# Moving PSUM copies to ScalarE and reordering work around the transposes in a fused attention and mixer kernel

## Chip, cores and metric

One NeuronCore of a Trainium2 chip. The metric is the device time of one execution in microseconds, median of repeated runs; all runs compared here are in the fast state (one single run, v_alone, can't be assigned); the granted TensorE clock is 0.99 to 1.00 of full speed in all of them.

## The reference

For 8 batches of 8 heads (sequence 576, head dimension 64) it computes causal attention with a bias made of a running sum, puts the heads together, and sends the result through a low-rank mixer over the sequence and a two-layer channel mixer:

```python
scores = q @ k.T / 8                                   # per batch and head
cum    = cumsum(max(s, 0))
scores = where(causal, -1e9, scores + minimum(-(cum_i - cum_j), 0))
x      = softmax(scores) @ v                           # heads side by side: [8, 576, 512]
u      = x + (x^T @ U @ V)^T                           # U: 576x32, V: 32x576
out    = u + relu(u @ w_ch1) @ w_ch2                   # 512 -> 2048 -> 512
```

## The kernel before

The work is cut into 32 pairs of heads; pairs 0 to 3 are batch 0, 4 to 7 batch 1, and so on. For a pair `n`, `T` transposes q and k on TensorE into PSUM, and four copies bring the result into an SBUF "slot"; `S` makes the scores and their exps, `V` the values. The channel mixer of an earlier group is cut into "chunks" of four 512-column matmuls, and `step_fill` slips them between the steps of attention so that TensorE always has something to do. An eviction, below, is a copy of a matmul's result out of PSUM, the memory that the matmuls of this kernel write to; exps and relus on ScalarE are evictions too.

The parts that matter here:

```python
ps_s = tile_pool(bufs=2, space=PSUM)   # pscore: two tiles of 1024 columns
ps_w = tile_pool(bufs=4, space=PSUM)   # pwork: four tiles of 512 columns, used in turn

def copies(n, hh, par):                # which engine copies a pair's transposes
    on_act = hh == 0 and (n in (0, 1, PB, PB + 1, PB + 3) or n == 2 and par == 0)  # PB = 4
    return nc.scalar.copy if on_act else nc.vector.tensor_copy

def transposes(n):                     # for b > 0: one yield for each head hh
    for hh in range(2):
        turn(hh, 0); turn(hh, 1)       # 8 transposes into one pwork tile
        for par in range(2):
            copies(n, hh, par)(dst[..., par], tp[par * D : par * D + D]...)   # 64x576 each
        yield
# ... cut ...
    step(M2)                           # M0..M3: the mixer of batch 0, one generator a head pair
    hidden_first(0)                    # hidden_first(kt): first four hidden tiles, step kt
    step(M3)
    hidden_first(1)
    step(M3)
    hidden_first(2)
    hidden_first(3)                    # ends with two 128x1024 relus on ScalarE (line 818)
    mix_first_end()
    in_program_order(tc, traced, [E.DVE, E.Activation, E.SP])
# ... cut ...
    for dt in range(4):                # V_sb and V_end: seven small copies on VectorE
        ...
    fill.append(chanmix(0, first_hT, 4))
    fill_with(3)                       # three chunks
    pace[1] = 8                        # from here one chunk at every second step
    weave("T4 T4 S4 T5 S4 T5 S4 S4")
    fill_with(5)
    pace[1] = 6
    weave("S5 S5 T6 S5 T6 S5 S6 R0 T7 S6 R1 T7 S6 R2 S6")   # R: v of batch 1, (act, dve) copies
```

The order in which TensorE runs its instructions is the order of the program text. The later order on VectorE and ScalarE is fixed at build time by a scheduler.

The softmax here doesn't subtract the row's maximum and nothing guards it: scores larger than these inputs give would overflow.

## Time and profile before

| | before |
|---|---|
| median | 382.94 us (382.32 to 383.56, 3 runs) |
| span of the profiled run | 381.3 us |
| TensorE busy | 371.3 us, 97% |
| VectorE busy | 223.6 us |
| ScalarE busy | 194.6 us |

From the page of the kernel before: the span, TensorE's busy line, the engines' shares of the chain that ended last, and the group of VectorE's slot copies (busy us and mean ns of one behind the first bar; behind the second, idle time before them and what ended it).

```profile
span 381.3 us, 8511 instructions
...
PE 371.3 (97%) x3583; PEld 210.8 (55%) x3583; DVE 223.6 (59%) x461; ACT 194.6 (51%) x292; POOL 65.1 (17%) x103
...
PE 85%; DVE 8%; ACT 3%; DMA 2%; issue 1%; SPq 0%; DVEq 0%; ACTq 0%
...
L310 DVE COPY slot<-pwork 64x576 bf16<-64x576 bf16 x117 | 93.6, 800 | 12.0 <-PE pwork L293 9.4
```

TensorE is the limit. But a matmul's recorded duration overlaps with the next one (the four at 111.88 us are recorded as 1.03 us long, and the next group starts after 0.87), so 97% busy hides gaps. The better measure is the time from one matmul's start to the next, less the rate at which matmuls of that size run when nothing is in the way. For that rate I took a line that fits the median spacings in the trace of the kernel before (216 ns at 512 columns, 135 at 320, 56 at 128, 29 at 64): N / 2.4 + 2.5 ns for N columns, at least 27 ns (32 columns take 25; without that floor the sum of waits below is 14.90 instead of 14.89). I call what lies above it (excesses over 20 ns) the PE waits. This stretch of the timeline gives the rate (start us, duration us, engine, line, operation, shapes, count): 64 matmuls of 512 columns in 13.81 us from first start to next group's start (322.97), 216 ns each.

```profile
309.16 13.98 PE L640 MATMUL pwork<-w_sb,hT 128*128 128x512 bf16 x64
```

Summed over a trace, by stretch of time:

| PE waits, us | 0-26 | 26-60 | 60-90 | 90-125 | rest | all |
|---|---|---|---|---|---|---|
| before | 5.28 | 3.30 | 2.74 | 1.26 | 2.31 | 14.89 |

The two waits that the change aims at look like this. First TensorE's, then ScalarE's timeline of the kernel before. In brackets stands the idle time of the engine and what ended it; that idle time starts at the modelled end of the matmul before, and so is shorter than the wait counted from starts (0.79 against 0.95 us here).

```profile
36.67 0.29 PE L293 MATMUL pwork<-identity,q_sd 72*128 72x72 bf16 x4
...
37.19 1.03 PE L630 MATMUL pwork<-uT,w_sb 128*128 128x512 bf16 x4
39.01 0.61 PE L375 MATMUL pscore<-slot 68*128 68x128 bf16 x6 [0.79 <-ACT slot L310]
```

```profile
33.66 1.94 ACT L818 ACTIVATE hT<-pscore 128x1024 bf16<-128x1024 f32 x2 [0.76 <-PE pscore L630]
...
37.37 1.59 ACT L310 COPY slot<-pwork 64x576 bf16<-64x576 bf16 x2
```

Pair 4's first transposes are done at 37.2 us, ScalarE copies them from 37.37 to 38.96, and the scores (line 375) start at 39.01. Later TensorE waits for VectorE's copies of pairs 8, 9 and 10, or for the evictions of x queued behind them. Five rows of TensorE's timeline of before:

```profile
68.70 0.62 PE L435 MATMUL pwork<-v_slot,hT 128*128 128x65 bf16 x15 [0.40 <-DVE slot L310]
...
75.27 1.04 PE L640 MATMUL pwork<-w_sb,hT 128*128 128x512 bf16 x4 [0.30 <-DVE slot L310]
...
77.52 0.62 PE L375 MATMUL pscore<-slot 68*128 68x128 bf16 x6 [0.28 <-DVE slot L310]
...
87.41 0.30 PE L293 MATMUL pwork<-identity,q_sd 72*128 72x72 bf16 x4 [0.15 <-DVE slot L310]
...
88.16 1.04 PE L630 MATMUL pwork<-uT,w_sb 128*128 128x512 bf16 x4 [0.32 <-DVE x_sb L445]
```

Counted from starts these five are 0.57, 0.46, 0.43, 0.31 and 0.48 us, 2.25 together.

The busy time of each engine from 60 to 90 us, for the kernel before (window in us; then PE, PEld, DVE, ACT, POOL busy us with counts; granted clock, DMA share, GB/s):

```profile
60.00:90.00 30.00, 28.55 (x399) 19.13 (x398) 25.16 (x55) 12.97 (x19) 4.19 (x6) 1.00 1.05 117
```

From 60 to 90 us VectorE is busy 25 of 30 us and ScalarE 13.

### The profile page before, as it was taken

The page shows a single profiled execution, that of the slowest core. Times are in us where ns is not written, and L with a number is a line of the kernel's source. Part 1 is how long each engine was busy: PE and PEld are TensorE (multiplying, and loading weights), DVE is VectorE, ACT ScalarE, POOL GpSimd, SP SyncE. Part 2 cuts the span into 40 slices and gives each one's busy share as a digit, 9 for nine tenths or more (in the row PEclk, how much of TensorE's full clock was granted, in tenths as well). Part 3 has the DMA queues.
Part 4 walks back from the last instruction along what each step waited for, and adds up shares of the span by engine and source line. Part 5 has one row for each costly group of instructions (what it writes and reads, how often), then busy time and mean ns, then how long its engine had stood idle before and what let it go on. Part 6 is the DMA issues. An engine that isn't in the chain of part 4 may idle for free.

```text
span 381.3 us, 8511 instructions
## 1 busy us (share of the span) xinstructions
PE 371.3 (97%) x3583; PEld 210.8 (55%) x3583; DVE 223.6 (59%) x461; ACT 194.6 (51%) x292; POOL 65.1 (17%) x103
## 2 busy tenths in 40 slices
PE   8899999999999999999999999999999999999997
PEld 3574456665665656555655665666555544444444
DVE  8883457977778776777668766786663132002002
ACT  3876985356642576247723774357542530630620
POOL 8995216005000600060006000000000000000000
PEclk9999999999999999999999999999999999999999
DMA  7999999937993994399239923320323032301002
GB/s 109 169 205 200 199 169 113 154 81 106 137 49 90 161 143 39 79 173 146 32 30 200 164 36 58 86 80 18 58 63 99 20 64 76 83 29 68 14 29 83
DMA packets 86110, 37.29 MB, mean 98 GB/s; under 512 B 66424, under 2 KB 80472, under 8 KB 86072
## 3 DMA queue, kind: packets, MB, share of 16 engines
q0 software_dynamic: 47216, 18.44, 49.0%
q1 hardware_dynamic: 38856, 18.31, 25.6%
q8 instruction: 28, 0.46, 0.5%
q14 instruction: 10, 0.08, 0.1%
HBM read 37.25 MB, written 9.70 MB: 123 GB/s over the span
## 4 chain that ended last, share of the span: by engine, by line
PE 85%; DVE 8%; ACT 3%; DMA 2%; issue 1%; SPq 0%; DVEq 0%; ACTq 0%
PE pwork L630 30%; PE pwork L640 29%; PE pscore L375 10%; PE pwork L435 6%; DVE slot L310 3%; PE pwork L293 3%; DVE x_sb L445 1%; ACT pT L390 1%; PE pscore L630 1%; PE pwork L677 1%; DMA slot<-hT 1%; DVE uT L489 1%; ACT slot L310 1%; DMA hT<-in_s_dram 1%; PE pwork L561 1%
## 5 line engine op out<-in xcount | busy, mean ns | idle before, releaser
L640 PE MATMUL pwork<-w_sb,hT 128*128 128x512 bf16 x560 | 135.4, 379 | 0.4 <-DVE slot L310 0.3
L630 PE MATMUL pwork<-uT,w_sb 128*128 128x512 bf16 x560 | 134.9, 379 | 0.6 <-DVE x_sb L445 0.3
L662 ACT ACTIVATE hT<-pwork 128x512 bf16<-128x512 f32 x140 | 84.3, 607 | 83.9 <-PE pwork L630 83.6
L310 DVE COPY slot<-pwork 64x576 bf16<-64x576 bf16 x117 | 93.6, 800 | 12.0 <-PE pwork L293 9.4
L390 ACT ACTIVATE pT<-pscore 128x1024 bf16<-128x1024 f32 x57 | 57.5, 1025 | 65.9 <-PE pscore L375 65.9
L630 PEld LDWEIGHTS <-w_sb 128*128 128x128 bf16 x576 | 50.9, 98 | 51.4 <-issue 1.8
L640 PEld LDWEIGHTS <-hT 128*128 128x128 bf16 x560 | 49.0, 98 | 50.1 <-issue 2.2
L700 DVE TENSOR_TENSOR o_sb<-pwork,u_sd 128x512 f32<-128x512 f32 x31 | 21.4, 691 | 64.8 <-PE pwork L640 63.7
L375 PE MATMUL pscore<-slot 68*128 68x128 bf16 (+1 forms) x506 | 54.9, 246 | 1.8 <-ACT slot L310 0.8
L375 PEld LDWEIGHTS <-slot 68*128 68x128 bf16 x570 | 41.8, 97 | 25.0 <-issue 1.5
L320 DVE TENSOR_TENSOR pT<-pT,keep 128x512 bf16<-128x512 bf16 (+1 forms) x81 | 28.6, 354 | 37.0 <-ACT pT L407 22.8
L435 PEld LDWEIGHTS <-pT 128*128 128x128 bf16 x870 | 32.4, 98 | 10.0 <-issue 0.3
L435 PE MATMUL pwork<-v_slot,pT 128*128 128x65 bf16 x870 | 34.6, 193 | 0.0
L401 ACT ACTIVATE pT<-pscore 128x1024 bf16<-128x1024 f32 x29 | 30.1, 1037 | 5.0 <-PE pscore L375 3.5
L445 DVE TENSOR_TENSOR x_sb<-pwork,rec 128x320 bf16<-128x320 f32 x64 | 31.3, 491 | 2.1
L108 POOL DMA_DIRECT2D q_sd<-in_q_dram x12 | 9.4, 783 | 125.1 <-PE pwork L293 116.9
L225 POOL DMA_DIRECT2D v_slot<-in_v_dram x24 | 21.4, 906 | 9.8 <-DMA w_sb<-in_moe_w_ch_dram 8.1
L444 DVE RECIPROCAL rec<-pwork 128x5 f32<-128x5 f32 x64 | 12.1, 191 | 15.9 <-PE pwork L435 15.3
L293 PEld LDWEIGHTS <-q_sd 72*128 72x128 bf16 x256 | 14.8, 98 | 10.9 <-DMA q_sd<-in_q_dram 0.9
L293 PE MATMUL pwork<-identity,q_sd 72*128 72x72 bf16 x256 | 18.0, 196 | 0.6 <-DMA q_sd<-in_q_dram 0.4
L293 PE MATMUL pwork<-identity,k_sd 72*128 72x72 bf16 x256 | 17.9, 197 | 0.1
L293 PEld LDWEIGHTS <-k_sd 72*128 72x128 bf16 x256 | 12.2, 98 | 1.0 <-DMA k_sd<-in_k_dram 0.7
(111 smaller groups left out, 199.2 us busy)
## 6 DMA issues: line engine op xcount, KB each, us to landing
out_dram<-o_sb SPq DMA_DIRECT2D x35, 256.0 KB
w_sb<-in_moe_w_ch_dram POOLq DMA_DIRECT2D x4, 1024.0 KB, 13.2
q_sd<-in_q_dram POOLq DMA_DIRECT2D x6, 576.0 KB, 9.1
k_sd<-in_k_dram POOLq DMA_DIRECT2D x6, 576.0 KB, 14.3
v_slot<-in_v_dram POOLq DMA_DIRECT2D x24, 128.0 KB, 15.6
hT<-in_v_dram POOLq DMA_DIRECT2D x2, 512.0 KB, 13.7
q_sd<-in_q_dram POOLq DMA_DIRECT2D x4, 144.0 KB, 5.2
k_sd<-in_k_dram POOLq DMA_DIRECT2D x4, 144.0 KB, 5.6
```

Of the source, the lines that this page charges most:

```text
L225: nc.gpsimd.dma_start(out=vt[:, t, :, 0:D], in_=v[b, :, ds(t * 128, 128), :].rearrange("h p d -> p h d"),)
L293: nc.tensor.transpose(tps[hh][:, c, t2, :], src[:, 2 * hp + hh, ds(t2 * 128, 128)], identity[:TP, :TP],)
L310: copies(n, hh, par)(dst[:, :, :, :, par], tp[par * D : par * D + D].rearrange("p c t m -> p c m t"),)
L320: nc.vector.tensor_tensor(dst, dst, keep[:, :, 0:w].to_broadcast([128, n_tiles, w]), op=ALU.min)
L375: nc.tensor.matmul(dst, lhsT=slot[0:KA, hh, ds(S + j * 128, 128)], rhs=slot[0:KA, hh, lo:hi], start=True, stop=True,)
L390: nc.scalar.activation(pT[:, hh, 0:1024], near, EXP, scale=scale)
L401: nc.scalar.activation(pT[:, :, 1024:1536], mid.rearrange("p (a b) -> p a b", a=2), EXP, scale=scale)
L435: nc.tensor.matmul(po[:, i, :], lhsT=pT[:, hh, ds(place(j, i), 128)], rhs=vt[:, j, h, :], start=(j == 0), stop=(j == i), skip_group_check= ...
L445: nc.vector.tensor_tensor(x_sb[:, hp, :, ds(hh * D, D)], po[:, :, 0:D], rec.to_broadcast([128, 5, D]), op=ALU.mult,)
L630: nc.tensor.matmul(f1, lhsT=w1_sb[:, kt, ds(nf * 128, 128)], rhs=u[:, kt, :], start=(kt == 0), stop=(kt == 3),)
L640: nc.tensor.matmul(f2, lhsT=hT[:, nf, ds(i * 128, 128)], rhs=w2_sb[:, nf, :], start=(nf == 0), stop=(nf == NF - 1 and not more), skip_grou ...
L662: nc.scalar.activation(hT[:, nf, :], f1, RELU)
```

## The change

Its intent: half of the slot copies of pairs 8 to 10, and all v copies of batch 1, go to ScalarE; three chunks go between pair 4's transposes and its scores to hide the copies; the first hidden step goes one place ahead; the V_sb copies are moved down in the text.

```diff
-        on_act = hh == 0 and (n in (0, 1, PB, PB + 1, PB + 3) or n == 2 and par == 0)
+        on_act = hh == 0 and (n in (0, 1, 4, 5, 7, 8, 9, 10) or n == 2 and par == 0)
...
-    step(M2)
     hidden_first(0)
-    step(M3)
+    step(M2, M3)
     hidden_first(1)
...
-    for dt in range(4):            # the V_sb and V_end copies
-        ...
-    fill_with(3)
-    pace[1] = 8
+    pace[1] = 0
...
-                    v_tiles(1, ((0, 1), (2, 3), (4,))[n], (act, dve))
+                    v_tiles(1, ((0, 1), (2, 3), (4,))[n], (act, act))
...
-    weave("T4 T4 S4 T5 S4 T5 S4 S4")
+    weave("T4 T4")
+    fill_with(3)
+    pace[1] = 8
+    weave("S4 T5 S4 T5 S4 S4")
+    for dt in range(4):            # the same V_sb and V_end copies
+        ...
     fill_with(5)
```

(Pairs 4, 5 and 7 were on ScalarE already: PB is 4.) One effect does not stand in the diff: before, the two T4 steps drew one chunk at the pace of 8, now they draw none. One chunk therefore comes later.

More of the change, by code (lines that the diff above doesn't have):

```diff
@@ L835 @@
     nc.gpsimd.memset(V_end, 0.0)
-    for dt in range(4):
-        if dt > 0:
-            nc.vector.tensor_copy(V_sb[ds(dt * R, R), :], V_sb[:R])
-        nc.vector.tensor_copy(V_end[ds(dt * R, R), dt, :], V_sb[:R, 512:S])
     def load(b):
@@ L868, in weave @@
             step_fill()
-    weave("T4 T4 S4 T5 S4 T5 S4 S4")
+    weave("T4 T4")
[3 more added lines that the diff above has]
+    for dt in range(4):
+        if dt > 0:
+            nc.vector.tensor_copy(V_sb[ds(dt * R, R), :], V_sb[:R])
+        nc.vector.tensor_copy(V_end[ds(dt * R, R), dt, :], V_sb[:R, 512:S])
     fill_with(5)
```

## The prediction

> **What bounds it.** TensorE. On the page PE is busy 371.3 of 381.3 us (97%); the chain of waits is 85% PE. Busy time flatters matmuls, so I priced gaps from starts in the timeline: 64 matmuls of 512 columns on the chain take 13.81 us, 216 ns each[...]. What starts exceed that rate by is about 15 us in all, some 5 before 20 us, which the change leaves alone. Between 26 and 90 us, where the edits lie, the losses above 0.1 us are:
>
> - 29.2: 0.34, the first mixing waits for DVE's ux; 30.1: 0.25, no cause shown
> - 39.0: 0.95, scores of pair 4 wait for ScalarE's slot copies (37.37 to 38.96)
> - 42.9: 0.20, for a relu
> - 57.2: 0.27, for an exp; 58.4: 0.77, for batch 1's v copy on DVE
> - 68.7: 0.57, 75.3: 0.46, 77.5: 0.43, 87.4: 0.31, 88.2: 0.48: DVE's slot copies of pairs 8, 9, 10, or x evictions queued behind them
>
> Together about 5 us, 1.3%: the ceiling. PE work doesn't change (7168 PE rows in both programs), so 2% is out of reach.
>
> **What the change does.**
> 1. The first hidden step goes ahead of the third mixing's second half: its four matmuls (0.86 us) cover the 0.34. Gain 0.3.
> 2. Pair 4's transposes come before the three chunks (12 matmuls, 2.6 us), which are to hide the copies (2 x 0.80 us on each engine). I expect this mostly to fail. [...] pair 4's copies stand behind the two 1.0 us relus of the first chunks: they end about 3.2 us after the transposes. The third chunk reuses the pwork buffer of pair 4's first transposes, so it waits about 0.9 us for ScalarE: the 0.95 moves from the scores to the third chunk. On DVE two V_sb copies (about 1 us) still stand before its slot copies. ScalarE idles only some 0.4 us between 33.7 and 45. Gain 0 to 0.4.
> 3. Batch 1's v copies all go to ScalarE (0.59 each against 0.69 on DVE). The second pair ends at about 58.2 instead of 58.4, behind an exp that doesn't move. Gain 0.2 to 0.4.
> 4. Pairs 8, 9, 10: half of the copies (6 x 0.80 us) move to ScalarE, busy only 3.6 to 5.2 us in each 10 from 60 to 90. A pair's copies now take 1.6 us instead of 3.2. Gain 1.6 to 2.1 of 2.25.
> 5. One chunk of the channel mixer falls to a later slot; that shifts every later phase: -0.5 to +0.3.
>
> Sum: about 2.3 us. Shorter DVE busy time alone is worth nothing.
>
> **Prediction.** 380.7 us, 8 in 10 between 379.2 and 382.4. Faster by over 2%: 0.01; within: 0.98; slower: 0.01.
>
> **What would show it.** DVE busy down by about 6 us, ScalarE up by as much. PE's waits at 68 to 88 us on slot copies gone. A wait of 0.5 to 1 us at a hidden chunk just before pair 4's scores, in place of that at the scores; a remaining wait at batch 1's last v tile.
>
> **What would make it wrong.** If pair 4's copies aren't held by the relus, step 2 gains 0.9: near 379.8. If relus delayed by slot copies starve pwork at 70 to 90 us, or shifted chunks make waits in later batches, the gain shrinks to nothing.

## The result

| | before | after |
|---|---|---|
| median | 382.77 us (4 runs) | 381.57 us (381.07 to 381.74, 4 runs) |
| span, profiled run | 381.3 | 380.0 |
| PE waits 0-26 us | 5.28 | 5.74 |
| 26-60 | 3.30 | 2.76 |
| 60-90 | 2.74 | 0.70 |
| 90-125 | 1.26 | 1.92 |
| rest | 2.31 | 2.35 |
| all | 14.89 | 13.48 |

The ratio is 0.9964 (95% interval 0.9945 to 0.9984): 1.4 us less, 0.6 to 2.1. Ratios here are the mean time of one kernel's runs over that of the other's runs of the same rounds, so not quite the ratio of the medians.

The first column of waits needs a word. Up to 26 us the program is the same in both kernels, and yet the waits there differ by 0.46 us. In the nine traces with all matmul records that I took they are between 4.62 and 6.77 us, mostly by when the first loads land (the wait at 12.5 to 13 us for a DMA into a slot is 0.79 us before and 1.34 after). A single run's time carries that noise, so for the profiles I compare the waits after 26 us: 9.61 before, 7.73 after, 1.88 less. The repeated runs' interval holds that number too. Of the 1.88, 0.25 is luck: the stall at 30.1 us of the kernel before, without a cause in the profile, is missing in copies_alone and v_alone, which run the same program there (see head_alone).

The page after, with the lines that answer to those of before, and ScalarE's slot copies:

```profile
span 380.0 us, 8508 instructions
...
PE 371.0 (98%) x3583; PEld 210.5 (55%) x3583; DVE 217.3 (57%) x453; ACT 199.8 (53%) x300; POOL 65.0 (17%) x103
...
PE 88%; ACT 6%; DVE 3%; DMA 2%; issue 1%; SPq 0%; ACTq 0%; DVEq 0%
...
L310 DVE COPY slot<-pwork 64x576 bf16<-64x576 bf16 x111 | 88.8, 800 | 12.3 <-PE pwork L293 10.0
...
L310 ACT COPY slot<-pwork 64x576 bf16<-64x576 bf16 x17 | 13.5, 797 | 1.4 <-PE pwork L293 1.2
```

```profile
60.00:90.00 30.00, 29.72 (x404) 20.09 (x403) 22.75 (x51) 19.50 (x27) 6.52 (x9) 1.00 1.12 125
```

VectorE is busy 6.3 us less and ScalarE 5.2 us more: eight copies have moved, and a slot copy takes as long on the one as on the other (800 and 797 ns). In the stretch from 60 to 90 us ScalarE's share has risen to 19.5 of 30 us, and TensorE's waits there have still fallen to 0.70 us.

Pair 4 after the change, TensorE and then ScalarE:

```profile
33.94 0.30 PE L293 MATMUL pwork<-identity,q_sd 72*128 72x72 bf16 x4
...
34.46 1.90 PE L630 MATMUL pwork<-uT,w_sb 128*128 128x512 bf16 x8
37.00 1.02 PE L630 MATMUL pwork<-uT,w_sb 128*128 128x512 bf16 x4 [0.64 <-ACT slot L310]
37.86 0.61 PE L375 MATMUL pscore<-slot 68*128 68x128 bf16 x6
```

```profile
33.53 1.94 ACT L818 ACTIVATE hT<-pscore 128x1024 bf16<-128x1024 f32 x2 [0.76 <-PE pscore L630]
35.35 1.60 ACT L310 COPY slot<-pwork 64x576 bf16<-64x576 bf16 x2
36.97 1.69 ACT L662 ACTIVATE hT<-pwork 128x512 bf16<-128x512 f32 x3
```

And VectorE's two copies of the same pair:

```profile
35.39 1.60 DVE L310 COPY slot<-pwork 64x576 bf16<-64x576 bf16 x2
```

The transposes now end at 34.5 us, but ScalarE is inside the two relus of line 818 until 35.4 and copies until 36.95. TensorE runs two of the three chunks (34.46) and waits 0.81 us with the third (37.00), whose pwork tile is the one that pair 4's first transposes still hold. The scores then follow without a wait. The 0.95 us has become 0.81.

Pairs 8 to 10, TensorE after:

```profile
67.02 1.07 PE L435 MATMUL pwork<-v_slot,hT 128*128 128x65 bf16 x30 [0.28 <-ACT slot L310]
...
73.34 1.03 PE L640 MATMUL pwork<-w_sb,hT 128*128 128x512 bf16 x4
...
75.38 0.60 PE L375 MATMUL pscore<-slot 68*128 68x128 bf16 x6
...
85.97 0.29 PE L293 MATMUL pwork<-identity,q_sd 72*128 72x72 bf16 x4
```

Of the five waits one is left, 0.45 us from starts, now for ScalarE's copies of pair 8.

At 113 us, in a part that the diff does not touch, a wait has grown. VectorE before and then TensorE before:

```profile
111.56 0.69 DVE L700 TENSOR_TENSOR o_sb<-pwork,u_sd 128x512 f32<-128x512 f32 x1
112.17 3.23 DVE L310 COPY slot<-pwork 64x576 bf16<-64x576 bf16 x4
115.43 0.29 DVE L473 CAST uxT<-pwork 128x128 bf16<-128x128 f32 x1
```

```profile
115.78 0.23 PE L477 MATMUL pwork<-identity,uxT 128*128 128x128 bf16 x1 [0.62 <-DVE uxT L473]
```

VectorE after and TensorE after:

```profile
108.76 3.26 DVE L310 COPY slot<-pwork 64x576 bf16<-64x576 bf16 x4 [0.40 <-PE pwork L293]
112.05 0.69 DVE L700 TENSOR_TENSOR o_sb<-pwork,u_sd 128x512 f32<-128x512 f32 x1
112.66 0.28 DVE L473 CAST uxT<-pwork 128x128 bf16<-128x128 f32 x1
```

```profile
113.00 0.23 PE L477 MATMUL pwork<-identity,uxT 128*128 128x128 bf16 x1 [0.90 <-DVE uxT L473]
...
117.83 0.29 PE L534 MATMUL pwork<-V_end,ux 128*128 128x64 bf16 x4 [0.21 <-DVE uT L489]
```

Before, the eviction of an output (line 700) went ahead of pair 14's four copies; after, it stands behind them, and the small copy uxT (line 473), for which TensorE waits, comes after both. The wait has grown from 0.79 to 1.07 us, and a second one of 0.38 us at 117.83 is new. At 50.1 us there is a third, 0.39 us, of an output chunk for the relu of the last hidden chunk. In the list of waits of the kernel after (idle time, so shorter than from starts) it is this one:

```profile
PE pwork L640 <- ACT hT L662: 0.2, 1, 0.2
```

### The profile page after: what moved, and what is told of

The parts are those of the page before. It is cut to its first block, busy times and chain, and to the rows that moved or that the text cites. A ratio compares the mean times of both kernels' runs of the same rounds, so it can differ in the third digit from the quotient of the medians.

```text
span 380.0 us, 8508 instructions
## 1 busy us (share of the span) xinstructions
PE 371.0 (98%) x3583; PEld 210.5 (55%) x3583; DVE 217.3 (57%) x453; ACT 199.8 (53%) x300; POOL 65.0 (17%) x103
## 4 chain that ended last, share of the span: by engine, by line
PE 88%; ACT 6%; DVE 3%; DMA 2%; issue 1%; SPq 0%; ACTq 0%; DVEq 0%
PE pwork L640 31%; PE pwork L630 30%; PE pscore L375 10%; PE pwork L435 8%; PE pwork L293 3%; ACT pT L390 1%; ACT slot L310 1%; ACT hT L662 1%; DMA slot<-hT 1%; PE pwork L677 1%; PE pscore L630 1%; PE pwork L464 1%; DVE uT L489 1%; DVE slot L310 1%; DMA hT<-in_s_dram 1%
## 5 line engine op out<-in xcount | busy, mean ns | idle before, releaser
L310 DVE COPY slot<-pwork 64x576 bf16<-64x576 bf16 x111 | 88.8, 800 | 12.3 <-PE pwork L293 10.0
L640 PEld LDWEIGHTS <-hT 128*128 128x128 bf16 x560 | 49.0, 98 | 50.2 <-issue 2.9
L435 PE MATMUL pwork<-v_slot,pT 128*128 128x65 bf16 x870 | 34.5, 194 | 0.0
L310 ACT COPY slot<-pwork 64x576 bf16<-64x576 bf16 x17 | 13.5, 797 | 1.4 <-PE pwork L293 1.2
```

What stands on the lines that cost most here:

```text
L310: copies(n, hh, par)(dst[:, :, :, :, par], tp[par * D : par * D + D].rearrange("p c t m -> p c m t"),)
L435: nc.tensor.matmul(po[:, i, :], lhsT=pT[:, hh, ds(place(j, i), 128)], rhs=vt[:, j, h, :], start=(j == 0), stop=(j == i), skip_group_check= ...
L640: nc.tensor.matmul(f2, lhsT=hT[:, nf, ds(i * 128, 128)], rhs=w2_sb[:, nf, :], start=(nf == 0), stop=(nf == NF - 1 and not more), skip_grou ...
```

## The experiments

Theory: the copies of pairs 8 to 10 carry the whole gain; the chunks move pair 4's wait instead of removing it, because ScalarE's order, fixed by the build, has two relus (1.94 us together) ahead of the copies; and the one deferred chunk costs about 1 us in three places. Rivals: the chunks carry the gain; VectorE or the number of buffers makes pair 4's wait; the later waits come from the copies on ScalarE or are noise. Eleven runs were made in three groups; each group had one chip, and the group's own runs of the kernel before beside it. All results were correct.

### copies_alone

```diff
 # the kernel before, with
-        on_act = hh == 0 and (n in (0, 1, PB, PB + 1, PB + 3) or n == 2 and par == 0)
+        on_act = hh == 0 and (n in (0, 1, 4, 5, 7, 8, 9, 10) or n == 2 and par == 0)
```

> The kernel before with one edit: half of the slot copies of pairs 8, 9 and 10 on ScalarE. Theory (the gain comes from here): of the 2.25 us of PE waits between 68 and 89 us at most 0.5 is left, nothing else changes, and the time falls by 1.5 to 2.0 us (ratio about 0.995): more than the whole change gained (1.37 us), since the other parts gave some back. Rival (the gain comes from the reordering of chunks, the copies only shorten DVE's busy time): under 0.5 us.

Measured: 380.91 us (380.42 to 381.17, 5 runs) against 382.69, ratio 0.9950 (0.9930 to 0.9971): 1.9 us less. PE waits from 60 to 90 us fell from 2.74 to 0.94; those for pair 4's scores (0.95), for batch 1's v copy (0.77) and for uxT (0.79) stayed. Waits after 26 us: 7.72 against 9.61, as much less as the runs. One part of the expectation was missed: of the 2.25 us not 0.5 at most is left but 0.67, at 67.5 us, for ScalarE's copies of pair 8. This one edit gives as much as the whole change or more.

### no_copies

```diff
 # the changed kernel, with
-        on_act = hh == 0 and (n in (0, 1, 4, 5, 7, 8, 9, 10) or n == 2 and par == 0)
+        on_act = hh == 0 and (n in (0, 1, PB, PB + 1, PB + 3) or n == 2 and par == 0)
```

> The changed kernel with the slot copies of pairs 8, 9, 10 all back on DVE, the rest of the change kept. Theory: the waits of 0.3 to 0.6 us between 66 and 88 us are back (about 2 us in all), and the time is that of before or a little more, 382.5 to 383.5. Rival (chunks carry the gain): about 381.5 to 382.

Measured: 382.80 us (six runs: five from 382.38 to 382.92, and one at 387.30 with a granted clock of 0.987) against 382.69. The ratio, with that one run in it, is 1.0015 (0.9978 to 1.0052); the medians are 0.1 us apart. The mean of the other five is within 0.2 us of that of the kernel before. Waits after 26 us: 9.71 against 9.61. The rest of the change is worth nothing by itself, as the theory said, but not because it does nothing. From 90 to 125 us there are 0.66 us more of waits, and from 60 to 90 us 0.71 less (2.03 against 2.74), since the shifted work already shortens the waits on pairs 8 to 10. On top of the rest, the copies therefore take away 1.33 us of waits (2.03 to 0.70) and not 1.8.

### chunks_alone

```diff
 # the kernel before, with only the change's move of fill_with(3), pace and weave("T4 T4"),
 # and of the V_sb copies
```

> The kernel before with one edit: pair 4's transposes ahead of the three chunks, and the V_sb copies moved down in the text. Theory: the 0.95 us wait at pair 4's scores becomes one of 0.8 to 0.9 at the third chunk, one chunk is deferred with its 0.39 us wait at 51 and the later ones, so the time does not fall: between 0.3 us less and 0.8 us more than before. Rival (the chunks hide the copies, as the author meant): 0.7 to 1.0 us less.

Measured: 383.91 us (383.56 to 384.08, 4 runs) against 382.72, ratio 1.0029 (1.0014 to 1.0044): 1.1 us more, 0.5 to 1.7. The rival is out, and my own range (up to 0.8 more) was missed by 0.3. In the trace pair 4's wait has moved to the third chunk (0.80 us), and all three waits of the deferred chunk are there: 0.40 at 50.2, 1.07 at 114.8, 0.38 at 119.7. Some of the waits on pairs 8 to 10 are a little shorter. This trace lacks 58 of 3583 matmul records, as do those of v_alone, pair14 and all_three; by the counts of each line all are of 512 columns, 56 of them after 26 us. An estimate that takes 216 ns off for each leaves about 9.9 us of waits after 26 us, 0.3 more than before. (For all_three the same estimate gives 5.9, and its complete twin all_three_again has 5.76.) So these waits account for some 0.3 of the 1.1 us, and where the rest comes from stays open. No run moved the V_sb copies alone.

### v_alone

```diff
-                    v_tiles(1, ((0, 1), (2, 3), (4,))[n], (act, dve))
+                    v_tiles(1, ((0, 1), (2, 3), (4,))[n], (act, act))
```

> The kernel before with one edit: batch 1's v copies all on ScalarE. Theory: of the 0.77 us that PE waits at 58.4 for the second pair's buffer about 0.2 goes, since the copies stand behind an exp that does not move (ends at 57.2 before and after); DVE busy 1.4 us less. Rival (the wait is DVE's alone): the wait goes whole.

Measured: one run, 382.66 us beside 382.72. The wait at 58 us is 0.53 instead of 0.77, now for ScalarE's copy; VectorE is busy 222.4 instead of 223.6. As the theory said: 0.24 of 0.77. The time of a single run shows nothing here; the result is the trace's.

### head_alone

```diff
-    step(M2)
     hidden_first(0)
-    step(M3)
+    step(M2, M3)
```

> The kernel before with one edit: the first hidden step goes ahead of the third mixing's second half. Theory: the 0.34 us wait for ux goes, nothing else changes; 0.2 to 0.6 us less than before (the upper end if the 0.25 at 30 us goes too). It is also needed for the sum: the parts measured alone should add up to the whole change (copies -1.8, chunks +1.2, v about -0.2, this about -0.5: -1.3 against -1.4 measured).

Measured: 382.38 us (381.99 to 382.68, 5 runs) against 382.76, ratio 0.9988 (0.9974 to 1.0001): 0.5 us less, not clear of zero. In the trace the 0.34 us wait is gone, and so is that of 0.25 at 30 us. The latter is not the edit's doing for sure: in the traces of no_copies and pair14, which run the same program as head_alone there, a wait of 0.65 and 0.64 us without any cause in the profile stands at 29.7 to 29.9. It comes and goes between runs, and I don't know what it is. In the traces of before, no_copies and pair14 it stands in front of the same place of TensorE's stream, the 351st recorded weight load, although that is line 630 in before and line 585 in the other two. So it goes with the place and not with the edit; no run tested why.

### turns_early

```diff
 # the changed kernel, with
     hidden_first(2)
+    T4 = transposes(4)
+    step(T4, T4)
     hidden_first(3)
...
-    weave("T4 T4")
```

> The changed kernel with the transposes of pair 4 one step earlier still, before the last hidden step, so that their two copies stand ahead of the two relus on ScalarE instead of behind them. Theory (ScalarE's fixed order, two relus of 1.0 us ahead of the copies, makes the third chunk wait 0.81 us for its pwork buffer): ScalarE's copies start at about 33 instead of 35.4, the 0.81 us wait goes, a wait of 0.2 to 0.6 us may stand at the chunk after pair 4's last scores, and the time falls by 0.4 to 0.8 us against the changed kernel. Rival (DVE's copies behind V_sb, or too few pwork buffers, make the wait): the third chunk still waits 0.5 us or more at 35 to 37.

Measured: 380.73 us (380.39 to 381.42, 5 runs) against 382.69, ratio 0.9945 (0.9926 to 0.9964), where the change itself had 0.9964 on another chip. ScalarE and TensorE of this kernel:

```profile
33.34 1.62 ACT L310 COPY slot<-pwork 64x576 bf16<-64x576 bf16 x2 [0.54 <-PE pwork L293]
34.98 1.94 ACT L818 ACTIVATE hT<-pscore 128x1024 bf16<-128x1024 f32 x2
```

```profile
34.50 2.75 PE L630 MATMUL pwork<-uT,w_sb 128*128 128x512 bf16 x12
37.09 0.61 PE L375 MATMUL pscore<-slot 68*128 68x128 bf16 x6
...
41.45 0.81 PE L630 MATMUL pwork<-uT,w_sb 128*128 128x512 bf16 x3 [0.40 <-ACT hT L662]
```

The copies start at 33.34, ahead of the relus. All three chunks run without a stop, 12 matmuls from 34.50 to 37.09, and so do the scores. By itself this does not part ScalarE from VectorE, for the edit put VectorE's two copies ahead of its V_sb copies too: they start at 33.60 here and at 35.39 in the changed kernel, where they end at 36.99, 0.04 us after ScalarE's. The program does part them. The third chunk takes the pwork tile of pair 4's first head, which ScalarE alone copies, and in the trace of the changed kernel its first matmul waits for semaphores of ScalarE and of TensorE itself, and for none of VectorE. So ScalarE's order was the cause, given four pwork tiles; no run had more. ScalarE is still full, though (its timeline lists no idle time from 33.34 to 42 us), and a wait for a relu of 0.56 us instead of 0.24 shows at 41.45. The net gain in waits from 26 to 60 us is 0.32 (2.76 to 2.43), just below the expected 0.4 to 0.8; by the medians it is 0.8, but on different chips and with intervals that overlap (0.9926 to 0.9964 against 0.9945 to 0.9984), so the time alone does not show a gain over the change.

### chunk_back

```diff
 # the changed kernel, with
-    fill_with(5)
+    fill_with(6)
     pace[1] = 6
```

> The changed kernel with six chunks instead of five after pair 4's scores, so that the one chunk which the change deferred is back before pair 5. Theory (the deferred chunk costs three waits later): the 0.39 us wait for a relu at 50 us goes; DVE's order at 110 us is that of before, with the output's eviction ahead of pair 14's copies, so the wait for uxT falls from 1.07 to about 0.8 and that of 0.38 at 118 goes. Together about 1.0 us less than the changed kernel, near 380.5. Rival (those waits come from the copies on ScalarE or from noise): the waits at 113 and 118 stay, no gain.

Measured: 380.18 us (379.64 to 380.23, 5 runs) against 382.69, ratio 0.9924 (0.9905 to 0.9943). VectorE of this kernel:

```profile
108.22 0.69 DVE L700 TENSOR_TENSOR o_sb<-pwork,u_sd 128x512 f32<-128x512 f32 x1
108.83 3.23 DVE L310 COPY slot<-pwork 64x576 bf16<-64x576 bf16 x4
112.09 0.29 DVE L473 CAST uxT<-pwork 128x128 bf16<-128x128 f32 x1
```

The eviction is ahead of the copies again, the wait at 112.4 is 0.79 as before the change, and those at 50 and 118 are gone. Waits after 26 us: 6.87 instead of 7.73. The deferred chunk had cost 1.05 us (0.39 + 0.28 + 0.38); a new 0.22 at pair 8's wait (0.67 instead of 0.45) takes some back, so that its net cost was 0.87 by the waits. The ratio lies below that of the change, and the intervals do not overlap.

### pair14

```diff
 # the changed kernel, with
-        on_act = hh == 0 and (n in (0, 1, 4, 5, 7, 8, 9, 10) or n == 2 and par == 0)
+        on_act = hh == 0 and (n in (0, 1, 4, 5, 7, 8, 9, 10, 14) or n == 2 and par == 0)
```

> The changed kernel with half of pair 14's slot copies on ScalarE too, which stands idle for 4 us just there. Theory (PE waits 1.07 us at 113 because uxT stands on DVE behind four copies and an eviction, 4.0 us in all): DVE reaches uxT 1.6 us earlier, the wait goes, and the time falls by about 1.0 us, unless the next wait on DVE takes part of it. Rival (uxT waits for TensorE or for ScalarE): the wait stays within 0.2 us.

Measured: 380.29 us (379.77 to 380.37, 4 runs) against 382.72, ratio 0.9933 (0.9918 to 0.9948). The wait of 1.07 us at 113 us is gone from the trace, that of 0.38 at 116.3 is still there. VectorE's queue was what uxT waited for.

### all_three

```diff
 # the changed kernel with turns_early, chunk_back and pair14 together
```

> The changed kernel with the three repairs together: pair 4's transposes before the last hidden step, six chunks, pair 14's copies halved. If the waits are independent the gains add up to 2.0 to 2.6 us: 379.0 to 379.6, about 0.99 of the kernel before. If one wait stands behind another, or the later phases move against us, less: 380 or more.

Measured: 378.78 us (378.51 to 379.57, 4 runs) against 382.72, ratio 0.9900 (0.9883 to 0.9916). That is 3.8 us less than before, and 2.8 below the changed kernel by the medians, where 2.0 to 2.6 had been expected from adding up. By the waits the three repairs are independent but for one overlap: singly they take away 0.33, 0.87 and 1.07 us, 0.28 of which (uxT) is counted twice, which leaves 1.99, and together they take away 1.97 (7.73 to 5.76, in all_three_again). The runs are too noisy to tell: singly the ratios add up to about 3.4 us, together they give 2.4. This version beats both kernels, by 1.0% and 0.7%.

### all_three_again

The same kernel, in the third group.

> The kernel with the three repairs once more, on the chip of pair8_split and head_alone, as their neighbour: 378.5 to 379.5, ratio to the kernel before 0.990.

Measured: 378.96 us (378.75 to 379.36, 4 runs) against 382.76, ratio 0.9902 (0.9888 to 0.9915). What TensorE still waited for between 26 and 125 us, from the list of waits of this run (total us, times, longest):

```profile
PE pwork L435 <- ACT slot L310: 0.5, 1, 0.5
...
PE pwork L630 <- ACT hT L662: 0.4, 1, 0.4
...
PE pscore L561 <- ACT v_slot L570: 0.4, 1, 0.4
```

Waits after 26 us: 5.76, against 9.61 before. The difference, 3.85 us, is the 3.8 us of the runs.

### pair8_split

```diff
 # all_three, with
-        on_act = hh == 0 and (n in (0, 1, 4, 5, 7, 8, 9, 10, 14) or n == 2 and par == 0)
+        on_act = par == 0 if n == 8 else hh == 0 and (n in (0, 1, 4, 5, 7, 8, 9, 10, 14) or n == 2 and par == 0)
```

> The kernel with the three repairs, and pair 8's copies split by rows instead of by head: each engine takes one of the two 0.8 us copies of each buffer. Theory (what is left of the wait at 67 us, 0.45 in the changed kernel and 0.67 in copies_alone and all_three, is the first transposes' pwork buffer, which ScalarE's two copies one after the other hold 1.6 us): the buffer comes free about 0.4 us sooner, that wait falls to 0.3 or less, and the time falls by 0.2 to 0.5 us against all_three. Rival (the wait is ScalarE's exp ahead of the copies, or DVE's eviction then becomes the last): unchanged or worse.

Measured: 379.14 us (378.71 to 380.35, 5 runs) against 382.76, ratio 0.9909 (0.9896 to 0.9922); its neighbour all_three_again had 0.9902. The wait itself fell as foreseen, from 0.67 to 0.25 us, but no gain of 0.2 to 0.5 us shows in the time. Its profiled run is its slowest, with 6.77 us of waits before 26 us and a granted clock of 0.995; the other four are at 378.71 to 379.21. Inconclusive on the time. One thing that I had not foreseen shows in VectorE's timeline:

```profile
67.77 0.81 DVE L310 COPY slot<-pwork 64x576 bf16<-64x576 bf16 x1 [0.39 <-ACT slot L310]
```

The copy on VectorE waited for that on ScalarE: both write interleaved columns of one slot, and the program orders them one after the other. So the two engines did not work at once on interleaved columns of one head. On the two heads of one slot they do: in the changed kernel pair 4's copies start at 35.35 on ScalarE and at 35.39 on VectorE.

## Why the prediction was right, and where it was off

Predicted were 380.7 us with a range of 379.2 to 382.4, and a gain of about 2.3 us. Measured were 381.57 and 1.4 us (1.9 by the waits after 26 us). By steps:

| step | predicted gain | measured | from |
|---|---|---|---|
| 1 hidden step ahead | 0.3 | 0.5 by runs, not clear of zero; the 0.34 wait is gone | head_alone |
| 2 chunks hide pair 4's copies | 0 to 0.4 | 0.10: 0.95 + 0.20 became 0.81 + 0.24 | trace after |
| 3 v copies | 0.2 to 0.4 | 0.24 | v_alone |
| 4 slot copies of pairs 8 to 10 | 1.6 to 2.1 | 1.9 by runs when alone; 2.25 of waits became 0.67, and 0.45 in the whole change | copies_alone, trace after |
| 5 deferred chunk | -0.5 to +0.3 | -1.05 in three waits (0.39 + 0.28 + 0.38), -0.87 net | trace after, chunk_back |

The mechanism was right in steps 1 to 4: where the gain comes from, that the chunks would only move pair 4's wait to the third chunk, and why. (Pair 4's copies ended 2.5 us after the transposes and not 3.2, and the wait was 0.81 and not 0.9.) Step 5 named no mechanism. That pair 4's copies would wait for the relus ahead of them on ScalarE was an estimate in the prediction; this case shows it as far as it goes: the slot copies start at 35.35 us, when the second relu ends, although their input was ready at 34.5; and turns_early removed the wait by changing nothing but the order of the work.

The mis-sized term is step 5: "One chunk of the channel mixer falls to a later slot; that shifts every later phase: -0.5 to +0.3". It was taken for noise around zero, and it was a loss, 1.05 us in three waits with nameable causes and 0.87 net. Two could have been read beforehand. The build's order of the changed kernel on VectorE had the eviction of line 700 behind pair 14's copies, in front of uxT, on which the trace of before already showed a wait of 0.79 us. And the output chunk that follows pair 5's scores needed a relu that now stood just before it. I had the list of both orders and looked only at the stretch that the diff touches.

My sentence on what would make the prediction wrong named this ("shifted chunks make waits in later batches"). That the range held proves little: it allowed any gain from 0.5 to 3.7 us. What also blurred the picture is that a single profiled pair differs by half a microsecond in the first 26 us for reasons that have nothing to do with the change.

## What to carry to other kernels

To hide a copy, look at what stands ahead of it in the copying engine's queue and which buffer its source holds: moving matmuls in between only helps until one of them needs that buffer (here the third chunk did, and 0.81 of the 0.95 us stayed), whereas moving the copy ahead in the queue took that wait of 0.81 us away here, though new waits left only 0.32 of it as gain. When work is drawn at a pace by a counter, a step moved across the counter changes the order everywhere behind it, on other engines too; compare the whole order, and put the drawn item back if it was not meant to move. On a kernel where one engine is 97% busy, price changes by the gaps between its starts, not by busy time: here they gave 1.89 us for copies_alone (1.9 by the runs) and 3.85 for the three repairs (3.8). They are not the whole: for chunks_alone they explain some 0.3 of 1.1 us. Nor do parts simply add: the copies are worth 1.8 us of waits alone and 1.33 on top of the rest.
